# Fused attention and expert layer: the first batch's opening rearranged (64-token guess, transposes moved, one product on GpSimd)

## The chip, the cores and the metric

The kernel runs on one core of one Trainium2 chip. The metric is device time in microseconds (us), the median over several executions. The trace shown comes from one further, profiled execution on the same core.

## The reference, cut to what matters

Eight batches (B = 8) of 576 tokens go through a memory-compressed attention and then through a layer with one expert per token. All arrays are float32.

```python
a = softmax(phi, axis=memory)                  # B,H,S,M = 8,8,576,32
k_m, v_m = a^T k, a^T v                        # 32 compressed keys and values per head, head_dim 64
attn = softmax(q k_m^T / 8, axis=memory)
x = (attn v_m) laid out as tokens x 512        # 4608 x 512
expert_idx = argmax(normalised x . normalised expert_emb / tau)   # of 8 experts
out = gate * relu(x @ w1[expert]) @ w2[expert] # 512 -> 1024 -> 512
```

## The kernel before, in words

Each batch is one pass through a long pipeline, and all engines follow an order written out by hand: an instruction stands in its engine's queue where the program emits it. TensorE (PE) does transposes and products, VectorE (DVE) and ScalarE (ACT) move results out of PSUM and do the softmaxes, GpSimd (POOL) computes low-order parts and weight splits, SyncE (SP) issues loads.

**Batch 0's opening** is in `moe_linformer` (from L1059). The softmax of `phi` is transposed (`turn`), the compressed keys and values are accumulated by `slots` (L544) and scaled into `ks` by `scale` (L569). `keys` (L578) transposes the keys into `kT`, `again` (L609) copies the keys once more behind the values in `ks`, and `values` (L613) transposes what stands there into `vT`. `score` (L632) multiplies keys with queries, 32 memory slots by tokens, into PSUM tiles `ts` (the first 128 tokens) and `tr` (the rest). The second softmax is worked in blocks of 32 tokens by 32 slots, held in `x`: `fill` (L61) transposes from PSUM, `weigh` (L67) takes the maximum, subtracts and exponentiates, `divide` (L78) sums, inverts and multiplies, `turn` (L89) transposes into `aw`. All of that but the exponential is on DVE.

The expert must be known before its weights can be loaded. So the kernel guesses it in batch 0 from the first 128 tokens (`first`, blocks 0 to 3): `squares` (L637) and `products` (L672) put values times values and values times expert embeddings into `vv`; `early` (L114) gives the experts' scores of those tokens, `best` the largest, `count` (L197) the votes, and `choose` (L205) reads the winner into a register and issues the load of `w1`. Meanwhile batch 1's `phi` softmax runs, and then the remaining 448 tokens (`others`, blocks 4 to 17) go through the same second softmax. What the guess got wrong is marked by `flags` and done again by a loop at the end (`rest`, L965).

`batch(0)` (L899) then emits `keys(1)` and `values(1)`, the first half of `project` (L708: the values times `w1` give `gh`, and by subtraction its low part `gl`), the copies `part` (L690: high part `ah` by ACT, low part `al` by POOL), `attend` (L109: 40 small products on PE, then DVE reductions and the choice per token), transposes `turned` (L163) and `norm` (L172), and starts the first layer.

**The first layer** (L723) makes 16 tiles `ph`: for each, six PE matmuls over `gh·ah, gh·al, gl·ah` of two groups g, an ACT activation into `hh` and a DVE subtraction into `hl`. A `ph` tile takes one of four PSUM buffers in rotation (`mm`, L401), so PE can't begin a tile before the tile four places earlier has been read by ACT and DVE. `project` and `turned` use the same rotation. Between tiles, the lists `first[n]` and `second[n]` of `steps` (L783) say which other work is emitted: in batch 0 the second half of `project` after tile 1, `turned(3, 4)` and the count `total` after tile 2, `norm`, the loads of batch 2, and after tile 9 batch 1's `scores`, which read `kT`.

`k.warm(n)` emits n products of constants on PE whose result nobody reads.

Of the kernel before, what the change touches and what calls it, by code (L numbers as in the profile page):

```python
# [47 lines left out]
class Tokens:  # L48
# [29 lines left out]
    def divide(self, gs, ks, apart=False):  # L78
        k, nc, b = self.k, self.nc, self.b
        x = k.x[:, gs[0] : gs[-1] + 1, ks]  # L80
        n = len(gs) * (ks.stop - ks.start)
        z = k.wk.tile([P, *x.shape[1:3]], F32, tag=f"z{n}", name=f"z{b}_{gs[0]}{ks.start}")
        for i in range(len(gs)) if apart else (slice(None),):
            nc.vector.tensor_reduce(out=z[:, i], in_=x[:, i], axis=AX.X, op=ALU.add)
        nc.vector.tensor_scalar(out=z, in0=z, scalar1=1e-9, scalar2=None, op0=ALU.add)
        nc.vector.reciprocal(out=z, in_=z)
        nc.vector.tensor_tensor(out=x, in0=x, in1=z.unsqueeze(3).broadcast_to(x.shape), op=ALU.mult)

# [24 lines left out]

    def early(self, i, po):  # L114

        k, nc = self.k, self.nc
        to = slice(T0[i], T0[i] + P)
        for g in range(NG):
            nc.tensor.matmul(po[:, 144 * g : 144 * g + P + E], lhsT=k.aw[:, g, to], rhs=k.vv[:, g], start=True, stop=True)
        e = po.rearrange("p (g m) -> p g m", g=NG)[..., D : D + E]  # L120
        nc.vector.tensor_reduce(out=self.lg[:, i], in_=e.rearrange("p g e -> p e g"), axis=AX.X, op=ALU.add)
        self.best(i)

# [29 lines left out]

    def best(self, *ti):

        k, nc = self.k, self.nc
        i = slice(ti[0], ti[-1] + 1)
        nc.vector.tensor_reduce(out=self.m[:, i], in_=self.lg[:, i], axis=AX.X, op=ALU.max)
        nc.vector.tensor_tensor(
            out=self.oh[:, i], in0=self.lg[:, i], in1=self.m[:, i].unsqueeze(2).broadcast_to((P, len(ti), E)), op=ALU.is_equal  # L160
        )

# [33 lines left out]

    def count(self, key, ti):  # L197

        for i in (-1, *ti):
            self.nc.tensor.matmul(  # L200
                key, lhsT=self.k.ones, rhs=self.k.eb if i < 0 else self.oh[:, i], start=i < 0, stop=i == ti[-1]
            )
        return key

    def choose(self, ti=range(NT)):  # L205

        k, nc, b = self.k, self.nc, self.b
        if b:
            self.key = self.all = key = self.all_at_once()
        else:  # L210
            key = self.pt([P, 512], "key")
            self.spare, key = key[:, E:], key[:, :E]
            self.key = self.all = self.count(key, ti)
# [73 lines left out]
class Kernel:  # L287
# [289 lines left out]

    def keys(self, b):  # L578

        ts = [self.pt([P, NG, P], f"tk{b}_{g}") for g in range(1 if b else NG)]  # L580
        for g in range(NG):
# [30 lines left out]

    def values(self, b, gs=range(NG), copy=None):  # L613

        t = self.pt([P, NG, P], f"tv{b}_{gs[0]}")
        for g in gs:
            self.nc.tensor.transpose(t[:, g], self.ks[:, g, D:], self.ident)
        for g in gs:
            x = t[:, g].rearrange("p (k m) -> p k m", k=2)
            for i in range(2):  # L620
                r, n = slice(64 * i, 64 * i + 64), slice(32 * (i ^ g), 32 * (i ^ g) + 32)
                (copy or (self.nc.vector.tensor_copy if b > 1 or g else self.nc.scalar.copy))(self.vT[b % 2][r, g, :, n], x[r, :, n])

    def heads(self, gs=range(NG)):
# [6 lines left out]

    def score(self, b, ts, lo, hi):  # L632

        for g, j, r, c, i in self.heads():
            self.nc.tensor.matmul(ts[g][j], lhsT=self.kT[b % 2][r, g, j], rhs=self.q(b, c)[r, lo:hi], start=True, stop=True)

    def squares(self, b, ts):  # L637

        vT = self.vT[b % 2]
        self.tail = ts  # L640
        for g, j, r, c, i in self.heads():
            k = c % 2
# [140 lines left out]
    def steps(self, b, t, u):  # L783
# [7 lines left out]
        if not b:  # L791
            late = t.late()
            first[0].append(lambda: t.norm(1))
            for g in range(NG):
                first[1].append(lambda g=g: self.part(g, slice(HS, S), self.nc.scalar.copy))
            first[1] += [lambda: t.norm(2), lambda: list(self.second_part)]
            first[2] += [lambda: t.turned(3, 4), t.total]
            first[3] += [lambda: t.norm(3, 4), lambda: self.load_kv(2)]
            for f in (4, 5, 6, 7):
                first[f].append(lambda: next(late))  # L800
            first[12] += [lambda: self.keep(0), lambda: self.load_q(2)]
# [97 lines left out]
    def batch(self, b, t, u):  # L899
# [16 lines left out]
        else:  # L916
            self.keys(1)
            self.values(1, copy=self.nc.scalar.copy)
            next(project)
            self.second_part = project  # L920
            for g in range(NG):
                self.part(g, slice(P, HS), self.nc.scalar.copy)
            t.attend()
            t.turned(1, 2)
            t.norm(0)
# [133 lines left out]
def moe_linformer(ctx, tc, phiT, qT, kv, kvt, emb, tau, w1, w2, out):  # L1059
# [28 lines left out]
    for ks in ((0, 1), (4,), (2,), (3,)):  # L1088
        k.slots(0, accs, ks=ks, first=0 in ks, last=3 in ks)
        if ks[0] < 3:  # L1090
            k.warm(2 if ks[0] == 2 else 1)
    k.scale(0)
    k.load_kv(1)
    k.keys(0)
    k.again()
    first, others = slice(0, 4), slice(4, BL)
    ts = [k.mm([P, P], f"ts0_{g}", 1 + g) for g in range(NG)]
    k.score(0, ts, 0, P)
    t.fill(range(NG), first, ts)
# [12 lines left out]
    t.early(0, k.mm([P, NC * (D + E)], "po0", 2))  # L1112
    e = t.choose((0,))
    t.turned(0, pt=k.pt)
    k.largest(1, 1)
    k.softmax(1, (1,))
    k.load_q(1, (0,))
    for i in (0, 4, 8):
        k.turn(1, i, min(i + 4, 9))
        k.turns += not i  # L1120
        if not i:
# [56 lines left out]
```

## Time and profile before

| what | value |
|---|---|
| median of 3 runs | 395.6 us (394.92 to 396.23) |
| profiled execution, own time | 395.72 us |
| its span, first to last instruction | 393.9 us |
| granted TensorE clock, mean | 1.00 of full speed |
| PE busy | 384.3 us (98%) |
| DVE busy | 244.3 us (62%) |
| ACT busy | 202.7 us (51%) |
| POOL busy | 186.8 us (47%) |

Busy shares are means over the whole span; the change touches only its first tenth. The rows further down are from the trace of this execution: a time line row gives the start and the duration in us, engine, line, operation, output, input, shape and how many instructions are merged in it; in brackets stands how long the engine sat idle before it and what released it.

### The profile page before, as it was taken

To read this page: it belongs to the slowest core of one execution; us is meant where nothing else is said; L and a number is where in the kernel's file an instruction comes from. 1 tells how busy PE (TensorE), PEld (TensorE's weight loads), DVE (VectorE), ACT (ScalarE), POOL (GpSimd) and SP (SyncE) were. 2 spreads that over 40 slices of the span, in tenths; PEclk is the share of its full clock that TensorE was granted. 3 is DMA by queue.
4 is the path that set the end of the run, shared out by engine and by line. 5 is a ranking of instruction groups with operands and counts; after the bars stand their busy time and mean duration, and the time that the engine had idled before them with its cause. 6 is when DMAs were issued, how large, how long until landed. Compare 5 with 4: busy or idle time off the path is not lost. (4 is left out here: it accounts for less than half of the span.)

```text
span 393.9 us, 10292 instructions
## 1 busy us (share of the span) xinstructions
PE 384.3 (98%) x3841; PEld 310.6 (79%) x3841; DVE 244.3 (62%) x810; ACT 202.7 (51%) x625; POOL 186.8 (47%) x229
## 2 busy tenths in 40 slices
PE   7899999999999999999999999999999999999994
PEld 3458878789787987879787987879788897879882
DVE  4698894689573798348961798538951596545000
ACT  5376732166284785657656675667641751145011
POOL 1036950596153941569051961559242871529300
PEclk9999999999999999999999999999999999999999
DMA  8999956996779937995489926996369505980011
GB/s 253 344 336 381 344 152 161 322 386 262 163 216 384 406 92 181 371 376 217 88 252 353 403 79 125 350 389 248 66 162 320 203 2 106 326 317 0 30 53 43
DMA packets 68710, 91.24 MB, mean 232 GB/s; under 512 B 41160, under 2 KB 46792, under 8 KB 68528
## 3 DMA queue, kind: packets, MB, share of 16 engines
q1 hardware_dynamic: 65408, 81.35, 62.5%
q0 software_dynamic: 2688, 8.26, 5.8%
q10 hardware_dynamic: 560, 0.93, 0.9%
q8 instruction: 31, 0.51, 0.5%
q14 instruction: 23, 0.19, 0.1%
HBM read 71.19 MB, written 19.33 MB: 230 GB/s over the span
## 5 line engine op out<-in xcount | busy, mean ns | idle before, releaser
L734 PE MATMUL ph<-aT,gh 128*128 128x288 f32 x512 | 103.1, 296 | 0.0
L774 PE MATMUL py<-wh,hh 128*128 128x512 f32 x256 | 100.9, 394 | 0.0
L774 PE MATMUL py<-wl,hh 128*128 128x512 f32 x256 | 99.7, 390 | 0.0
L774 PE MATMUL py<-wh,hl 128*128 128x512 f32 x256 | 99.7, 390 | 0.0
L705 POOL TENSOR_TENSOR wl<-w2s,wh 128x512 fp32r<-128x512 f32 x64 | 83.3, 1302 | 5.1
L734 PEld LDWEIGHTS ph<-aT,gh 128*128 128x128 f32 x512 | 81.8, 188 | 1.8 <-DVE hl L741 0.8
L734 PE MATMUL ph<-aT,gl 128*128 128x288 f32 x256 | 75.4, 295 | 0.0
L738 ACT ACTIVATE hh<-ph 128x224 fp32r<-128x224 f32 (+1 forms) x128 | 48.7, 387 | 35.1 <-PE ph L734 34.6
L741 DVE SCALAR_TENSOR_TENSOR hl<-ph,hh 128x224 fp32r<-128x224 f32 (+1 forms) x128 | 51.8, 417 | 22.7 <-ACT hh L738 16.2
L779 ACT ACTIVATE ys<-py,gate 128x512 f32<-128x512 f32 (+1 forms) x40 | 25.7, 643 | 73.2 <-PE py L774 42.4
L945 POOL DMA_DIRECT2D out_dram<-ys x28 | 16.3, 582 | 92.2 <-ACT ys L779 83.5
L774 PEld LDWEIGHTS py<-wh,hh 128*128 128x128 f32 x256 | 48.1, 188 | 11.1 <-issue 1.4
L774 PEld LDWEIGHTS py<-wh,hl 128*128 128x128 f32 x256 | 48.1, 188 | 10.2
L774 PEld LDWEIGHTS py<-wl,hh 128*128 128x128 f32 x256 | 48.1, 188 | 9.4
L734 PEld LDWEIGHTS ph<-aT,gl 128*128 128x128 f32 x256 | 48.0, 188 | 0.0
L718 DVE TENSOR_TENSOR gl<-pg,gh 128x512 fp32r<-128x512 f32 x32 | 19.9, 683 | 41.1 <-ACT gh L717 41.1
L704 POOL CAST wh<-w2s 128x512 fp32r<-128x512 f32 x62 | 41.4, 668 | 0.1
L695 POOL TENSOR_TENSOR aT<-aw,aT 128x576 fp32r<-128x576 f32 (+3 forms) x20 | 23.8, 1207 | 34.0 <-DVE aT L694 27.9
L763 PE MATMUL py<-w2s,h 128*64 128x256 f32 x256 | 29.4, 382 | 0.0
L539 ACT COPY eT<-xt 32x256 f32<-32x256 f32 x64 | 25.8, 403 | 1.1
L763 PEld LDWEIGHTS py<-w2s,h 128*64 128x64 f32 x256 | 17.7, 137 | 10.4 <-DVE aw L95 1.8
L606 ACT COPY kv<-kt 32x64 f32<-32x64 f32 x80 | 19.4, 243 | 5.3 <-DVE kt L596 4.4
(168 smaller groups left out, 467.5 us busy)
## 6 DMA issues: line engine op xcount, KB each, us to landing
kx<-kv SPq DMA_DIRECT2D x32, 512.0 KB, 10.2
w2s<-w SPq DMA_DIRECT2D x28, 512.0 KB, 10.0
w1s<-w SPq DMA_DIRECT2D x28, 512.0 KB, 6.7
out_dram<-ys POOLq DMA_DIRECT2D x28, 256.0 KB, 6.3
qt<-qT SPq DMA_DIRECT2D x12, 576.0 KB, 9.5
ad<-aw SPq DMA_DIRECT2D x8, 576.0 KB, 11.4
td<-x SPq DMA_DIRECT2D x56, 72.0 KB, 2.5
ea<-td SPq DMA_DIRECT2D x7, 512.0 KB, 4.0
```

The lines of the kernel that those rows point to most:

```text
L539: nc.scalar.copy(eT[to, :8, m].rearrange("p (g k) m -> p g k m", g=NG), xt[at, :, q : BL - 2 : 4])
L606: nc.scalar.copy(y, self.kt[32 * l : 32 * l + 32, g, h + 2 * i :: 2 - 4 * i])
L695: self.nc.gpsimd.tensor_tensor(out=al, in0=a, in1=ah.bitcast(F32), op=ALU.subtract)
L704: (copy or self.nc.scalar.copy)(h, x)
L705: self.nc.gpsimd.tensor_tensor(out=l, in0=x, in1=h.bitcast(F32), op=ALU.subtract)
L718: nc.vector.tensor_tensor(out=self.gl[:, g, f], in0=ps[g], in1=self.gh[:, g, f].bitcast(F32), op=ALU.subtract)
L734: nc.tensor.matmul(p, lhsT=w[:, g, fs], rhs=x[:, g, to], start=g == 0 and k == 0, stop=g == 1 and k == 2)
L738: nc.scalar.activation(self.hh[:, f, at], q, AF.Relu)
L741: nc.vector.scalar_tensor_tensor(out=self.hl[:, f, at], in0=q, scalar=0.0, in1=self.hh[:, f, at].bitcast(F32), op0=ALU.max, op1=ALU.subtract)
L763: nc.tensor.matmul(p[64 * j : 64 * j + 64], lhsT=self.h4[:, f], rhs=self.w2s[:, f, d * j : d * j + d], start=f == 0, stop=f == 7,)
L774: nc.tensor.matmul(p, lhsT=h[:, f, to], rhs=w[:, f], start=f == 0 and k == 0, stop=f == 7 and k == 2)
L779: nc.scalar.activation(y[:, :d], p, AF.Copy, scale=gate[:, i : i + 1])
```

## The change

The first guess uses 64 tokens in place of 128, so `first` has 2 blocks and `others` 16. The keys' second copy (`again`) and the transposes of batch 0's values now stand directly behind the transposes of its keys, ahead of the scores. The router's transposes move from behind the scores to behind `slots` of the third key block, with one dummy product fewer there, and three fewer ahead of `divide`. `turned(0)` leaves the opening. `divide` of the others is emitted ahead of `again` for batch 1, and its second product (group 1) goes to GpSimd. In `batch(0)` the keys and values of batch 1 are no longer turned ahead of the first layer but after its tile 1, in one PSUM buffer of the rotation; the rest of the high and low parts (columns 64 to 288) stands ahead of `project`; `turned` and `norm` go by other token tiles and later places.

```diff
     def divide(self, gs, ks, apart=False):
...
-        nc.vector.tensor_tensor(out=x, in0=x, in1=z.unsqueeze(3).broadcast_to(x.shape), op=ALU.mult)
+        for i in parts:
+            y = x[:, i]
+            (nc.gpsimd if i == 1 else nc.vector).tensor_tensor(
+                out=y, in0=y, in1=z[:, i].unsqueeze(y.ndim - 1).broadcast_to(y.shape), op=ALU.mult
+            )
...
+    def keys_values(self, b):
+        room = self.mm([P, 2, NG, P], f"tkv{b}")
+        self.keys(b, lambda shape, name: room[:, 0])
+        self.values(b, copy=self.nc.scalar.copy, room=lambda shape, name: room[:, 1])
...
             first[0].append(lambda: t.norm(1))
             for g in range(NG):
-                first[1].append(lambda g=g: self.part(g, slice(HS, S), self.nc.scalar.copy))
-            first[1] += [lambda: t.norm(2), lambda: list(self.second_part)]
-            first[2] += [lambda: t.turned(3, 4), t.total]
-            first[3] += [lambda: t.norm(3, 4), lambda: self.load_kv(2)]
-            for f in (4, 5, 6, 7):
+                first[0].append(lambda g=g: self.part(g, slice(HS, S), self.nc.scalar.copy))
+            first[1] += [lambda: list(self.second_part), lambda: self.keys_values(1)]
+            first[3].append(lambda: self.load_kv(2))
+            first[4] += [lambda: t.turned(2, 3), lambda: t.turned(4), t.total]
+            first[5].append(lambda: t.norm(2, 3, 4))
+            for f in (5, 6, 7, 8):
                 first[f].append(lambda: next(late))
...
-            self.keys(1)
-            self.values(1, copy=self.nc.scalar.copy)
+            for g in range(NG):
+                self.part(g, slice(64, HS), self.nc.scalar.copy)
             next(project)
             self.second_part = project
-            for g in range(NG):
-                self.part(g, slice(P, HS), self.nc.scalar.copy)
             t.attend()
-            t.turned(1, 2)
+            t.turned(0, 1)
             t.norm(0)
...
         k.slots(0, accs, ks=ks, first=0 in ks, last=3 in ks)
+        if ks[0] == 2:
+            next(router, None)
         if ks[0] < 3:
-            k.warm(2 if ks[0] == 2 else 1)
+            k.warm(1)
     k.scale(0)
+    k.again()
     k.load_kv(1)
     k.keys(0)
-    k.again()
-    first, others = slice(0, 4), slice(4, BL)
-    ts = [k.mm([P, P], f"ts0_{g}", 1 + g) for g in range(NG)]
-    k.score(0, ts, 0, P)
+    k.values(0, copy=k.nc.scalar.copy)
+    first, others, few = slice(0, 2), slice(2, BL), slice(0, 64)
+    ts = [k.mm([P, 64], f"ts0_{g}", 1 + g) for g in range(NG)]
+    k.score(0, ts, 0, 64)
     t.fill(range(NG), first, ts)
-    next(router, None)
-    k.values(0, copy=k.nc.scalar.copy)
-    ts = [k.mm([P, S - P], f"tr0_{g}", g) for g in range(NG)]
-    k.score(0, ts, P, S)
-    k.squares(0, [k.pt([P, D + E], f"tl0_{g}") for g in range(NG)])
+    ts = [k.mm([P, S - 64], f"tr0_{g}", g) for g in range(NG)]
+    tl = [k.pt([P, D + E], f"tl0_{g}") for g in range(NG)]
+    for g in range(NG):
+        k.score(0, ts, 64, S, (g,))
+        k.squares(0, tl, (g,))
     list(t.weigh(range(NG), first))
     k.products(0)
-    k.warm(5, 2)
+    k.warm(2, 2)
     t.divide(range(NG), first)
     t.turn(range(NG), first)
...
-    t.early(0, k.mm([P, NC * (D + E)], "po0", 2))
-    e = t.choose((0,))
-    t.turned(0, pt=k.pt)
+    t.early(k.mm([P, NC * (D + E)], "po0", 2), few)
+    e = t.choose(few)
...
-        k.part(g, slice(0, P), k.nc.scalar.copy)
+        k.part(g, few, k.nc.scalar.copy)
...
     k.scale(1)
+    t.divide(range(NG), others, True)
     k.again(k.nc.gpsimd.tensor_copy)
-    t.divide(range(NG), others, True)
     t.turn(range(NG), others)
```

## Rows read from the trace of the kernel before

**Rows 1.** Busy time by stretch (PE, PEld, DVE, ACT, POOL, clock, DMA), first layer.

```profile
31.20:43.00 11.80, 11.80 (x135) 9.99 (x134) 9.84 (x42) 7.39 (x20) 8.70 (x12) 1.00 1.03 347
```

**Rows 2.** Page, costliest groups: one of the second layer's three products.

```profile
L774 PE MATMUL py<-wh,hh 128*128 128x512 f32 x256 | 100.9, 394 | 0.0
```

**Rows 3.** Time line, PE from batch 1's last key block to the first layer.

```profile
24.62 0.16 PEld L557 LDWEIGHTS acc0t<-kx,eT 128*32 128x32 f32 x8 [0.36 <-DMA kx<-kv]
...
26.81 0.40 PEld L582 LDWEIGHTS tk<-ident,ks 128*128 128x128 f32 x2 [0.25 <-ACT ks L574]
...
27.79 1.09 PE L715 MATMUL pg<-w1s,kv 64*32 64x512 f32 x16
...
30.07 0.73 PE L136 MATMUL po<-vv,aw 64*64 64x72 f32 x33
...
31.15 0.51 PE L734 MATMUL ph<-aT,gh 128*128 128x288 f32 x2
```

**Rows 4.** Time line, 14 to 20 us: the chain to the guess.

```profile
14.68 0.69 PE L635 MATMUL ts<-qt,kv 64*32 64x128 f32 x16
...
15.16 0.58 DVE L65 STREAM_TRANSPOSE x<-ts 128x128 f32<-128x128 f32 x2
...
15.63 0.44 PE L617 MATMUL tv<-ident,ks 128*128 128x128 f32 x2
...
16.11 0.90 ACT L622 COPY kv<-tv 64x64 f32<-64x64 f32 x4 [0.18 <-PE tv L617]
16.24 0.42 DVE L74 TENSOR_TENSOR x<-x,mx 128x256 f32<-128x256 f32 x1
...
17.03 0.42 ACT L76 ACTIVATE x<-x 128x256 f32<-128x256 f32 x1
...
19.30 0.70 PE L119 MATMUL po<-vv,aw 128*128 128x136 f32 x4 [0.50 <-DVE aw L93]
```

**Rows 5.** DVE instructions by form, to 48 us (busy us, mean ns, idle before).

```profile
L84 DVE TENSOR_REDUCE z<-x 128x14 f32<-128x448 f32 x2 | 1.1, 603 | 0.0
...
L84 DVE TENSOR_REDUCE z<-x 128x8 f32<-128x256 f32 x1 | 0.4, 421 | 0.8 <-ACT x L76 0.8
```

**Rows 6.** Time line, 25 to 31 us: the other tokens' softmax on DVE, ACT's copies.

```profile
25.42 0.17 DVE L505 RECIPROCAL rs<-rs 128x2 f32<-128x2 f32 x1 [0.38 <-POOL rs L501]
...
27.28 1.09 DVE L87 TENSOR_TENSOR x<-x,z 128x896 f32<-128x896 f32 x1
...
28.92 1.07 ACT L717 CAST gh<-pg 128x512 fp32r<-128x512 f32 x2 [0.16 <-PE pg L715]
...
29.63 0.20 DVE L95 STREAM_TRANSPOSE aw<-x 128x64 f32<-128x64 f32 x1
29.76 1.25 DVE L718 TENSOR_TENSOR gl<-pg,gh 128x512 fp32r<-128x512 f32 x2
29.88 0.56 ACT L694 CAST aT<-aw 128x160 fp32r<-128x160 f32 x2
```

**Rows 7.** Time line, 47 to 53 us: DVE and POOL with two SBUF inputs each.

```profile
47.71 0.75 DVE L74 TENSOR_TENSOR x<-x,mx 128x576 f32<-128x576 f32 x1
47.82 1.78 POOL L705 TENSOR_TENSOR wl<-w2s,wh 128x512 fp32r<-128x512 f32 x1
...
49.97 2.52 POOL L705 TENSOR_TENSOR wl<-w2s,wh 128x512 fp32r<-128x512 f32 x2
...
51.41 1.70 DVE L74 TENSOR_TENSOR x<-x,mx 128x576 f32<-128x576 f32 x1
```

**Rows 8.** Time line, the first layer's opening: DVE subtractions, moved transposes, fourth tile.

```profile
32.66 0.46 DVE L741 SCALAR_TENSOR_TENSOR hl<-ph,hh 128x288 fp32r<-128x288 f32 x1
...
34.82 0.60 PE L169 MATMUL tt<-ident,aw 128*128 128x128 f32 x4
...
35.43 0.54 PE L734 MATMUL ph<-aT,gh 128*128 128x288 f32 x2
```

**Rows 9.** Time line, PE weight loads of batch 1's scores.

```profile
41.18 0.12 PEld L635 LDWEIGHTS ts<-sT,kv 64*32 64x32 f32 x4 [0.17 <-DMA ex<-phiT]
```

More of the change, by code (lines that the diff above doesn't have):

```diff
@@ L82, in divide @@
         z = k.wk.tile([P, *x.shape[1:3]], F32, tag=f"z{n}", name=f"z{b}_{gs[0]}{ks.start}")
-        for i in range(len(gs)) if apart else (slice(None),):
+        parts = range(len(gs)) if apart else (slice(None),)
+        for i in parts:
             nc.vector.tensor_reduce(out=z[:, i], in_=x[:, i], axis=AX.X, op=ALU.add)
@@ L86, in divide @@
         nc.vector.reciprocal(out=z, in_=z)
-        nc.vector.tensor_tensor(out=x, in0=x, in1=z.unsqueeze(3).broadcast_to(x.shape), op=ALU.mult)
+        for i in parts:
+            y = x[:, i]
+            (nc.gpsimd if i == 1 else nc.vector).tensor_tensor(
+                out=y, in0=y, in1=z[:, i].unsqueeze(y.ndim - 1).broadcast_to(y.shape), op=ALU.mult
+            )
     def turn(self, gs, ks):
@@ L112, in attend, with early @@
         self.pairs()
-    def early(self, i, po):
+    def early(self, po, to):
         k, nc = self.k, self.nc
-        to = slice(T0[i], T0[i] + P)
         for g in range(NG):
[L119 to L122, printed above, removed]
+            nc.tensor.matmul(po[to, 144 * g : 144 * g + P + E], lhsT=k.aw[:, g, to], rhs=k.vv[:, g], start=True, stop=True)
+        e = po[to].rearrange("p (g m) -> p g m", g=NG)[..., D : D + E]
+        nc.vector.tensor_reduce(out=self.lg[to, 0], in_=e.rearrange("p g e -> p e g"), axis=AX.X, op=ALU.add)
+        self.best(0, to=to)
     def open(self):
@@ L152, in pairs, with best @@
         self.best(*range(NT))
-    def best(self, *ti):
+    def best(self, *ti, to=slice(P)):
         k, nc = self.k, self.nc
         i = slice(ti[0], ti[-1] + 1)
[L158 to L161, printed above, removed]
+        lg, m = self.lg[to, i], self.m[to, i]
+        nc.vector.tensor_reduce(out=m, in_=lg, axis=AX.X, op=ALU.max)
+        nc.vector.tensor_tensor(out=self.oh[to, i], in0=lg, in1=m.unsqueeze(2).broadcast_to(lg.shape), op=ALU.is_equal)
     def turned(self, *ti, pt=None):
@@ L195, in all_at_once, with count, choose @@
         return key
[L197 to L202, printed above, removed]
+    def count(self, key, to):
+        self.nc.tensor.matmul(key, lhsT=self.k.ones, rhs=self.k.eb, start=True, stop=False)
+        self.nc.tensor.matmul(key, lhsT=self.k.ones[to], rhs=self.oh[to, 0], start=False, stop=True)
         return key
-    def choose(self, ti=range(NT)):
+    def choose(self, to=None):
         k, nc, b = self.k, self.nc, self.b
@@ L212, in choose @@
             self.spare, key = key[:, E:], key[:, :E]
-            self.key = self.all = self.count(key, ti)
+            self.key = self.all = self.count(key, to)
         ki = k.wk.tile([1, 1], I32, tag="ki", name=f"ki{b}")
@@ L576, in scale, with keys @@
                 self.nc.vector.tensor_scalar(out=to, in0=self.accs[g], scalar1=r, scalar2=None, op0=ALU.mult)
-    def keys(self, b):
-        ts = [self.pt([P, NG, P], f"tk{b}_{g}") for g in range(1 if b else NG)]
+    def keys(self, b, room=None):
+        ts = [(room or self.pt)([P, NG, P], f"tk{b}_{g}") for g in range(1 if b else NG)]
         for g in range(NG):
@@ L611, in again, with values @@
         (copy or self.nc.vector.tensor_copy)(self.ks[:, :, 2 * D :], self.ks[:, :, :D])
-    def values(self, b, gs=range(NG), copy=None):
-        t = self.pt([P, NG, P], f"tv{b}_{gs[0]}")
+    def values(self, b, gs=range(NG), copy=None, room=None):
+        t = (room or self.pt)([P, NG, P], f"tv{b}_{gs[0]}")
         for g in gs:
@@ L630, in heads, with score, squares @@
                 yield g, slice(l, l + 32), slice(64 * i, 64 * i + 64), c, slice(n, n + 32)
-    def score(self, b, ts, lo, hi):
-        for g, j, r, c, i in self.heads():
+    def score(self, b, ts, lo, hi, gs=range(NG)):
+        for g, j, r, c, i in self.heads(gs):
             self.nc.tensor.matmul(ts[g][j], lhsT=self.kT[b % 2][r, g, j], rhs=self.q(b, c)[r, lo:hi], start=True, stop=True)
-    def squares(self, b, ts):
+    def squares(self, b, ts, gs=range(NG)):
         vT = self.vT[b % 2]
         self.tail = ts
-        for g, j, r, c, i in self.heads():
+        for g, j, r, c, i in self.heads(gs):
             k = c % 2
@@ L1119, in moe_linformer @@
         k.turn(1, i, min(i + 4, 9))
-        k.turns += not i
+        k.turns += i == 4
         if not i:
```

## The prediction

> **What bounds the kernel now.** I first read the busy time by stretch. From the first layer on, PE has no free time: 11.80 us busy in the 11.80 us from 31.20 on, at the full granted clock (1.00, the 2.4 GHz level) [rows 1], and the second layer's products have no idle time ahead of them [rows 2]. So the change can gain only by starting the first layer earlier, and each PE instruction that it carries past that start costs its own time.
>
> The second view is the time line of PE ahead of that start [rows 3]. At 24.62 PE waits for batch 1's last key block. After its products and ACT's scaling come the transposes of keys and values (26.81 to 27.79), the first half of `project` (27.79), the products of `attend`, and tile 0 at 31.15. PE has one wait worth naming here: the products of group 1 go on at 30.07, and what they need is DVE's last transpose, ended at 29.63 + 0.20 = 29.83 [rows 3, 6]. Two chains thus end together: PE's from the key block, and DVE's through the other tokens' softmax. Moving batch 1's transposes shortens the first by 27.79 - 26.81 = 0.98 us, so PE alone allows tile 0 at 30.17. The second must be shortened as well, and that I work out next. From DVE's end to tile 0 it is 31.15 - 29.83 = 1.32 us, the same work before and after (four transposes of tokens, the rest of `attend`).
>
> **The guess chain, from 14.7 us.** The reader is to see in [rows 4] that the scores start at 14.68, the fills at 15.16, and that the exponential starts at 17.03 although the subtraction ended at 16.24 + 0.42 = 16.66: ACT was copying values until 16.11 + 0.90 = 17.01. After the change the value transposes (0.44) stand ahead of the scores, partly in PE's wait for the copied keys; I take 0.25 of delay (ends 0 and 0.44). Scores of half the width give back some 0.08, the two fills of 64 columns 0.09 each (0.58 for two of 128 against 0.20 for one of 64 [rows 4, 6]), so the maximum starts when it did. The price per element is (603 - 421) / 192 = 0.95 ns [rows 5]; maximum, subtraction, sum, product and exponential each lose 128 elements, 0.12 us, 0.6 together. The wait behind the value copies (0.37) goes, because those copies now lie ahead of the fills. The transposes into `aw` give 0.09. Sum: 1.05 us earlier (ends 0.8 and 1.1); PE's `early` products go from 19.30 to 18.25. The dropped dummy products stood in PE's waits; the router's transposes take the place of one of them while PE waits for a key block, so both are costed at nothing (cover gone: some 0.4 us for the four).
>
> **The other tokens' chain.** Everything DVE does next is queued behind it and moves up by 1.05. But 64 more elements per group pass through two fills, maxima, subtractions and sums: 8 x 0.06 = 0.5 us. Of DVE's wait of 0.38 for POOL's part of the row sums [rows 6] I take 0.15 as gone (ends 0 and 0.38), since DVE arrives later relative to POOL. The product then starts at 27.28 - 1.05 + 0.5 - 0.15 = 26.6.
>
> What is a product on POOL worth? [rows 7] show the two engines shutting each other out when both have two SBUF inputs: POOL's split needs 2.52 / 2 = 1.26 but 1.78 when DVE's subtraction is running, and went on for 1.14 after that ended (48.46 to 49.60); DVE's subtraction needs 0.75 but 1.70 when it meets POOL's. The change's two products are of just that kind and become ready at the same reciprocal. DVE has no semaphore to wait for and should be first: 0.42 + 256 x 0.95 ns = 0.66, to 27.25. POOL's follows, to 28.4. DVE meanwhile turns group 0 (one turn is (29.83 - 28.37) / 2 = 0.73, plus 0.06 for the added columns, 0.79, to 28.05), waits 0.35 for POOL, and turns group 1 until 29.2. With both products on DVE it would be 26.6 + 1.21 + 2 x 0.79 = 29.4. So the move to POOL is worth 0.2 us, and if the engines did not exclude each other POOL would be done at 27.9 and DVE at 28.85.
>
> The Trainium skill ("GPSIMD Engine Reference", sections 1, Specifications, and 4.1, Engine selection) names contention with VectorE instructions of two SBUF inputs and advises VectorE for elementwise two-input work, GpSimd being about twice as slow. By that advice the sum would stand at 29.4 in place of 29.2; the trace agrees on the contention (1.70 against 0.75 us) and here the advice is worth less than nothing only because DVE has transposes to do meanwhile.
>
> DVE's end thus moves from 29.83 to 29.2, tile 0 from 31.15 to **30.55, 0.6 us earlier** (ends 0.98, PE's own limit above, and a delay of 0.3, the POOL rival below).
>
> **What is carried past the start.** Six transposes now lie in the PE-bound part: two each of keys and values, and the two of the token tile that the opening used to turn. Four cost 0.60 busy [rows 8], 0.15 each at the most; since runs overlap I take 0.11 each: **+0.65** (ends 0.4, if some fall into waits, and 0.9). ACT's copies, the norms and POOL's splits move too; their engines have idle time per tile, and where that fails is a rival below.
>
> **New waits.** ACT now has the two `part` copies (0.28 each for 160 columns) queued ahead of the `gh` copies (0.54 each) [rows 6], and the second of them waits for DVE's last large transpose, at about 29.0. So `gh` of group 0 is ready at 29.9 and DVE, which went straight from its transposes to `gl` at 29.76, sits idle for 0.7. `gl` ends at 31.15 against 29.76 + 1.25 = 31.01; behind it are queued the reductions of `attend`, `norm(0)` and `hl` of tile 0, which goes from 32.66 to 32.8. Tile 0 itself is 0.6 earlier, so PE meets buffers that DVE hasn't released: I take **+0.2** of waiting for tile 2's buffer (ends 0 and 0.8). On the other side the scores of batch 1 wait 0.17 for a load [rows 9]; they now come later and the load is issued earlier: **-0.17** (ends 0 and -0.17).
>
> **Sum.** -0.6 + 0.65 + 0.2 - 0.17 = +0.1 us against the profiled execution's 395.72 (span 393.9 and 1.8 around it, 0.1 above the median of 395.6): **395.8 us**, no change. About 0.3%, 1.2 us, is what a measurement of this kernel can tell from none.
>
> **Rivals.**
> - *Faster.* The opening gains all that PE allows (-0.98), because my DVE prices are too high or the engines share better than in [rows 7], and the six transposes and the buffer waits cover each other (0): -0.98 - 0.17 = -1.15, 394.5 us. For it: DVE at 28.85 without exclusion would make PE's limit the later one. Against it: PE showed no waits in the first layer that transposes could fill [rows 1].
> - *Slower: ACT becomes the bound of tiles 2 to 5.* The copies of batch 1's keys and values move into the layer behind two wide `part` copies and two `gh` copies. They are four value copies of 0.90 together [rows 4] and one key copy of about 0.37 (0.28 for 160 columns, 96 more at the price of 0.95 ns [rows 5, 6]). If ACT has no idle time there, `hh` of tile 2 is late by all of it, 1.27 us, and PE stands still at the tile four places on: 395.8 + 1.27 = 397.1. It decides if `hh` of tile 2 ends later than PE reaches tile 6. Against it: the rotation leaves four tiles of slack.
> - *POOL first.* If POOL's product gets the shared input ahead of DVE's, DVE's starts 1.26 later: DVE's end is 26.6 + 1.26 + 0.66 + 1.58 = 30.1, 0.9 later than forecast, and the time 396.7. For it: the release is the same instant. Against it: in [rows 7] the engine already running kept it, and DVE is in sequence.
> - *The guess fails.* If 64 tokens named another expert than 128, batch 0 would be done again by the closing loop, about (393.9 - 31.15) / 8 = 45 us. The second layer's 256 products are 8 batches by 4 full tiles by 8 slices [rows 2], so no batch was repeated and all tokens of a batch go to one expert; 64 tokens give the same one.
>
> **How the numbers follow.** The forecast has 0.46 (its own range 395.1 to 396.6), the faster rival 0.2, ACT 0.21, POOL first 0.12, the failed guess 0.01. The faster rival is centred on the bound of 0.3%, so I count 0.16 as faster; of ACT's case all but 0.02 is beyond it on the other side, and POOL first adds 0.02 with the higher price of the transposes: slower 0.22, same 0.62. The range that leaves out two in ten reaches from 394.4 into the faster case to 397.3 with ACT's.
>
> **What would show it.** Right: `early` on PE near 18.25; POOL's product starting when DVE's ends and lasting to about 28.4; DVE's last `aw` transpose ending near 29.2; tile 0 near 30.55 with the clock still at 1.00; tile 5 at about the time it had before. Wrong: tile 0 earlier than 30.2 or later than 31.2; a PE wait over 0.5 us between tiles 2 and 6; any second-layer product beyond 256.

## The result and the profile after

The change made the kernel slower: a median of 398.3 us (396.82 to 398.51, 6 runs) against 395.68 us (394.92 to 396.51, 6 runs), a ratio of 1.0057 with a 95% interval of 1.0037 to 1.0077. A second series, e7 below, gave 397.89 us (12 runs) against 396.33 us, 1.0046 (1.0026 to 1.0066). The forecast was 395.8 us with a range to 397.3; the result lies above it.

The profiled execution took 397.67 us, its span is 395.9 us. I start where the forecast started, with the first layer's stretch by busy time (columns: PE, PEld, DVE, ACT, POOL, granted clock, DMA share, GB/s), here of the changed kernel:

```profile
31.20:43.00 11.80, 10.70 (x117) 8.93 (x123) 7.42 (x33) 7.82 (x23) 8.56 (x11) 1.00 1.04 357
```

PE, busy all of this stretch before [rows 1], now has 1.1 us without work, at the same clock. The list of PE's waits from the end of the opening to the second layer (in total, times, longest, us) says where:

```profile
PE tkv L618 <- ACT kv L588: 1.1, 1, 1.1
PE pg L722 <- DMA w1s<-w: 0.3, 1, 0.3
PE po L140 <- issue: 0.2, 1, 0.2
PE py L770 <- DVE hl L748: 0.2, 1, 0.2
```

The largest stands inside the new function. The time line of the changed kernel around it:

```profile
32.97 0.44 PE L583 MATMUL tkv<-ident,ks 128*128 128x128 f32 x2
33.10 1.07 ACT L724 CAST gh<-pg 128x512 fp32r<-128x512 f32 x2 [0.46 <-PE pg L722]
...
34.06 0.39 ACT L588 COPY kv<-tkv 128x256 f32<-128x256 f32 x1
...
34.51 0.20 PEld L618 LDWEIGHTS tkv<-ident,ks 128*128 128x128 f32 x2 [1.34 <-ACT kv L588]
34.51 0.44 PE L618 MATMUL tkv<-ident,ks 128*128 128x128 f32 x2 [1.10 <-ACT kv L588]
...
34.70 0.51 PE L741 MATMUL ph<-aT,gh 128*128 128x288 f32 x2
```

Keys are transposed at 32.97. The values' transposes go into the same PSUM buffer, and the program has ACT's copy of the keys (L588) between the two; so they wait for that copy, and in ACT's queue it stands behind both `gh` copies. Tile 2 follows at 34.70, 4.51 us after tile 0; before it was 2.77 us (31.15 to 33.92), without that wait:

```profile
33.92 0.53 PE L734 MATMUL ph<-aT,gh 128*128 128x288 f32 x2
```

The opening, in the same time line:

```profile
12.73 0.35 DVE L577 TENSOR_SCALAR ks<-acc0t,rs 128x128 f32<-128x128 f32 x1 [1.31 <-PE acc0t L558]
...
17.31 0.65 PE L123 MATMUL po<-vv,aw 128*64 128x136 f32 x4
...
25.45 0.69 DVE L90 TENSOR_TENSOR x<-x,z 128x512 f32<-128x512 f32 x1
25.50 1.55 POOL L90 TENSOR_TENSOR x<-x,z 128x512 f32<-128x512 f32 x1 [0.60 <-DVE z L87]
...
26.82 1.09 PE L722 MATMUL pg<-w1s,kv 64*32 64x512 f32 x16 [0.35 <-DMA w1s<-w]
...
27.72 0.20 DVE L100 STREAM_TRANSPOSE aw<-x 128x64 f32<-128x64 f32 x1
...
29.25 0.60 PE L140 MATMUL po<-vv,aw 64*64 64x72 f32 x22 [0.19 <-issue]
...
30.19 0.51 PE L741 MATMUL ph<-aT,gh 128*128 128x288 f32 x2
```

These times can't be set against those of before as they stand. The scaling of batch 0's keys, the first of these rows, starts anywhere from 12.73 to 14.98 us in the 13 profiles of this document, and the rest of the opening moves with it; in the kernel before it starts at

```profile
13.59 0.35 DVE L576 TENSOR_SCALAR ks<-acc0t,rs 128x128 f32<-128x128 f32 x1 [1.35 <-PE acc0t L557]
```

I therefore count the opening from that instruction. `early` then comes 5.71 us after it before (19.30 - 13.59) and 4.58 after: 1.13 earlier. DVE's last transpose ends 16.24 after it before and 15.19 after (27.92 - 12.73): 1.05 earlier. But tile 0 comes 17.56 after it before and 17.46 after: 0.1 earlier. The gain that DVE made stopped ahead of PE.

The one other place that differs is far behind, in batch 1's second layer of the changed kernel:

```profile
106.52 1.72 PE L558 MATMUL acc<-kx,eT 128*32 128x128 f32 x51
108.77 0.64 PE L558 MATMUL acc<-kx,eT 128*32 128x128 f32 x13 [0.53 <-issue]
```

From the half tile ahead of this to the next batch's first projection the changed kernel took 24.76 us (101.51 to 126.27), the kernel before 23.86 (100.42 to 124.28): 0.9 us in a wait that the profile ascribes to nothing. The half tile that ends the first layer starts, first in the changed kernel, then in the kernel before, at

```profile
48.53 3.67 PE L770 MATMUL py<-w2s,h 128*64 128x256 f32 x32 [0.16 <-DVE hl L748]
```

```profile
47.43 3.67 PE L763 MATMUL py<-w2s,h 128*64 128x256 f32 x32
```

The balance of the two spans: tile 0 at 30.19 against 31.15 (-0.96, of which 0.86 is the early arrival), tile 0 to the half tile 18.34 us against 16.28 (+2.06), this wait (+0.9): +2.0, the difference of 395.9 and 393.9.

### The profile page after: what moved, and what is told of

The parts are those of the page before. It is cut to its first block, busy times and chain, and to the rows that moved or that the text cites. A ratio compares the mean times of both kernels' runs of the same rounds, so it can differ in the third digit from the quotient of the medians.

```text
span 395.9 us, 10286 instructions
## 1 busy us (share of the span) xinstructions
PE 384.5 (97%) x3837; PEld 310.4 (78%) x3837; DVE 243.1 (61%) x810; ACT 202.8 (51%) x625; POOL 188.2 (48%) x230
```

## The experiments

The table holds, for each kernel's profile, the start of batch 0's scaling, of the first half of `project`, of tile 0 and of the half tile that ends the first layer; "opening" is from scaling to tile 0, "layer" from tile 0 to the half tile. The last column is the ratio to the kernel before, timed with it on the same chip. Each row is one profiled execution. Two pairs have the same order in the opening, the changed kernel and e7, e6 and e9: their openings differ by 0.59 and 0.30 us, and the time from scaling to `project` by 0.67 and 0.69. A smaller difference between two openings is thus no finding. The layer repeats far better: 18.34, 18.35 and 18.35 in the changed kernel, e7 and e4.

| kernel | scaling | project | tile 0 | half tile | opening | layer | ratio (95%) |
|---|---|---|---|---|---|---|---|
| before | 13.59 | 27.79 | 31.15 | 47.43 | 17.56 | 16.28 | 1 |
| changed | 12.73 | 26.82 | 30.19 | 48.53 | 17.46 | 18.34 | 1.0057 (1.0037 to 1.0077) |
| changed, again (e7) | 14.00 | 27.42 | 30.87 | 49.22 | 16.87 | 18.35 | 1.0046 (1.0026 to 1.0066) |
| e1 transposes first | 13.59 | 27.47 | 31.60 | 48.94 | 18.01 | 17.34 | 1.001 (0.9995 to 1.0024) |
| e2 old place | 13.31 | 28.28 | 31.13 | 47.92 | 17.82 | 16.79 | 1.0017 (1.0003 to 1.0031) |
| e3 move alone | 14.98 | 28.97 | 32.54 | 50.38 | 17.56 | 17.84 | 1.0035 (1.001 to 1.0061) |
| e4 product on DVE | 13.09 | 26.88 | 30.32 | 48.67 | 17.23 | 18.35 | 1.0048 (1.0026 to 1.0069) |
| e5 PE stream shifted | 13.62 | 27.18 | 32.93 | 50.26 | 19.31 | 17.33 | 1.0051 (1.0029 to 1.0072) |
| e6 old place, again first | 13.19 | 27.39 | 30.78 | 47.42 | 17.59 | 16.64 | 1.0001 (0.9983 to 1.002) |
| e8 guess alone | 13.96 | 28.48 | 31.35 | 48.12 | 17.39 | 16.77 | 1.001 (0.9993 to 1.0026) |
| e9 e6, old tiles | 13.37 | 28.26 | 31.26 | 47.96 | 17.89 | 16.70 | 1.0001 (0.9988 to 1.0015) |
| e10 before, less load | 12.79 | 26.70 | 31.14 | 47.41 | 18.35 | 16.27 | 0.9989 (0.9974 to 1.0004) |
| e11 e6, less load | 13.47 | 26.59 | 29.98 | 47.10 | 16.51 | 17.12 | 0.9983 (0.9969 to 0.9997) |

**e1: the four transposes ahead of their copies.** Same buffer, same instructions, another order on PE.

```diff
     def keys_values(self, b):
-        room = self.mm([P, 2, NG, P], f"tkv{b}")
-        self.keys(b, lambda shape, name: room[:, 0])
-        self.values(b, copy=self.nc.scalar.copy, room=lambda shape, name: room[:, 1])
+        nc, room = self.nc, self.mm([P, 2, NG, P], f"tkv{b}")
+        for n, c in enumerate((slice(0, 2 * D), slice(D, 3 * D))):
+            for g in range(NG):
+                nc.tensor.transpose(room[:, n, g], self.ks[:, g, c], self.ident)
+        nc.scalar.copy(self.kT[b % 2], room[:, 0])
...
```

> The changed kernel, but batch 1's four transposes of keys and values are issued before any copy out of their shared PSUM buffer. Theory A (the values' transposes stand behind ACT's copy of the keys, which stands behind the two gh copies): PE's wait of 1.10 us ahead of them goes, tile 2 starts some 3.4 us after tile 0 instead of 4.5, and the time falls by about 1.1 us to 397.2. Rival B (ACT is the bound of these tiles, the wait only moves to the next buffer): less than 0.3 us is won, PE waits for hh or hl at tiles 2 to 6 instead. The wait of 0.5 to 0.9 us in batch 1's second layer (behind the 51st of 64 key products, near 108 us) is untouched by either.

The layer went from 18.34 to 17.34 us, by 1.00, and the time to 1.001 of before, from 1.0046 and 1.0057. In the time line the four transposes run without a break, and the next tile follows while ACT is still busy with `gh`:

```profile
34.38 0.66 PE L630 MATMUL tkv<-ident,ks 128*128 128x128 f32 x4
34.52 1.08 ACT L731 CAST gh<-pg 128x512 fp32r<-128x512 f32 x2 [0.47 <-PE pg L729]
34.79 0.51 PE L748 MATMUL ph<-aT,gh 128*128 128x288 f32 x2
...
35.47 0.39 ACT L631 COPY kv<-tkv 128x256 f32<-128x256 f32 x1
```

This is theory A. ACT copies the keys as late as before, 3.87 us after tile 0 in both kernels, and PE doesn't wait for it; so rival B, ACT as the bound, falls. The time, 396.76 us, is 0.4 below what theory A gave. Separate buffers for keys and values, with the order left as it was, would test the same from the other side; that was not run. The profile holds a wait that is not in theory A, and it hides part of the gain in this one execution:

```profile
30.66 0.60 PE L140 MATMUL po<-vv,aw 64*64 64x72 f32 x22 [0.96 <-issue]
```

Within `attend` (40 products, which leave 80 rows in the trace) PE stops behind the 58th row, where the changed kernel stops for 0.19 us; see e5.

**e2: batch 1's keys and values in their old place.**

```diff
-            first[1] += [lambda: list(self.second_part), lambda: self.keys_values(1)]
+            first[1] += [lambda: list(self.second_part)]
...
+            self.keys(1)
+            self.values(1, copy=self.nc.scalar.copy)
             for g in range(NG):
                 self.part(g, slice(64, HS), self.nc.scalar.copy)
             next(project)
```

> The changed kernel with batch 1's keys and values turned ahead of the first half of project again, as before; all else as changed. Theory A: the 1.10 us wait and 0.4 us of transposes leave the first layer, while tile 0 starts up to 1.0 us later; net 0.5 to 1.2 us faster than the changed kernel, 397.1 to 397.8. Rival C (the opening is bound by DVE or by the w1 load, not by PE): tile 0 starts no more than 0.4 us later, and the time is 396.7 or less. Rival B: no change, 398.3.

396.49 us, below what theory A gave and in the range of rival C: the layer is 1.55 us shorter than the changed kernel's, while the opening is 0.4 to 0.95 us longer (17.82 against 17.46 and 16.87). So the move buys the opening less than it costs the layer. The opening also has a wait of its own making:

```profile
26.08 1.55 POOL L90 TENSOR_TENSOR x<-x,z 128x512 f32<-128x512 f32 x1 [0.60 <-DVE z L87]
27.58 0.28 POOL L612 COPY ks<-ks 128x128 f32<-128x128 f32 x1
27.91 0.44 PE L618 MATMUL tv<-ident,ks 128*128 128x128 f32 x2 [0.83 <-POOL ks L612]
```

The keys' second copy (L612) stands behind POOL's product in POOL's queue, and PE's value transposes wait for it. In the changed kernel the same copy is late too, but nothing needs it before the first layer.

**e3: the move alone, in the kernel before.**

```diff
...
-            self.keys(1)
-            self.values(1, copy=self.nc.scalar.copy)
             next(project)
...
-            first[1] += [lambda: t.norm(2), lambda: list(self.second_part)]
+            first[1] += [lambda: t.norm(2), lambda: list(self.second_part), lambda: self.keys_values(1)]
```

> The kernel before, with nothing but batch 1's keys and values moved behind tile 1 in one buffer, as in the change. Theory A: DVE's chain still sets tile 0 (31.15), the first layer gains 0.4 us of transposes and a wait of about 1 us: 397.1, 1.4 us slower than before. Rival C: tile 0 moves up by what PE is relieved of (0.98) and the time stays within 0.5 us of before. Rival B: as A, but with waits for hh spread over tiles 2 to 6.

397.74 us against 396.22: 1.5 us slower, as theory A had it. The layer grew by 1.56 us and the opening is the same 17.56. Two waits stand in its trace:

```profile
28.97 1.09 PE L721 MATMUL pg<-w1s,kv 64*32 64x512 f32 x16 [0.81 <-DMA w1s<-w]
...
36.85 0.44 PE L617 MATMUL tkv<-ident,ks 128*128 128x128 f32 x2 [1.10 <-ACT kv L587]
```

The second is that of the changed kernel. The first shows where the 0.98 us went by which the move relieves PE ahead of `project`: PE waits 0.81 of it for `w1`. The move alone costs 1.0035, its interval reaching to 1.0061, the whole change 1.0046 and 1.0057: about as much, so the rest of the change comes to little.

**e4: both products on DVE.**

```diff
-            (nc.gpsimd if i == 1 else nc.vector).tensor_tensor(
+            nc.vector.tensor_tensor(
```

> The changed kernel with both second products of divide on DVE. Theory: in the changed kernel tile 0 waits for the load of w1 and the products behind it, not for DVE's last transposes, so 0.2 to 0.5 us more on DVE is hidden: 398.3, no change. Rival D (POOL's product buys what it looks like, because DVE's opening sets tile 0 and its hl): 0.3 to 0.8 us slower, 398.6 to 399.1. The wait near 108 us tells, by being there or not, whether it is a matter of this one profile.

1.0048 against 1.0046 and 1.0057: no difference. The products and the last transpose on DVE are here

```profile
25.97 1.29 DVE L90 TENSOR_TENSOR x<-x,z 128x512 f32<-128x512 f32 x2
...
28.53 0.20 DVE L100 STREAM_TRANSPOSE aw<-x 128x64 f32<-128x64 f32 x1
```

From the first product's start to DVE's end it is 2.76 us (25.97 to 28.73) against 2.47 with POOL's product (25.45 to 27.92), so the product on POOL frees 0.29 us on DVE, and tile 0 doesn't come later for lack of it: the opening, 17.23 us, lies between the two of the changed kernel. Rival D falls. With the same order on PE, batch 1's second layer has no wait near 108 us here.

**e5: 24 tiny products ahead of `early`.** Added to e1, where PE is idle.

```diff
+    tiny = k.mm([P, 4], "tiny", 2)
+    for _ in range(24):
+        k.nc.tensor.matmul(tiny, lhsT=k.ones, rhs=k.ones[:, :4], start=True, stop=True)
     t.early(k.mm([P, NC * (D + E)], "po0", 2), few)
```

> The kernel of the reordered transposes (batch 1's four transposes ahead of their copies) with 24 tiny products of constants added on PE ahead of early, where PE is idle. Theory P (the wait behind the 58th of the 80 rows of attend, 0.96 us there and released by nothing the profile shows, hangs on the place in PE's instruction stream): with 48 instructions more ahead of it the wait leaves attend and falls on the last key products of batch 1, where PE waits for w1 anyway; tile 0 starts 0.2 to 1.0 us earlier relative to the first products' arrival, time 396.0 to 396.7. Rival Q (it is a hidden dependency of those products): the wait stays behind the 58th row and the time is the same, 396.8, or later by the 24 products' 0.6 us.

```profile
28.21 0.87 PE L140 MATMUL po<-vv,aw 64*64 64x72 f32 x34
31.61 0.97 PE L140 MATMUL po<-vv,aw 64*64 64x72 f32 x46 [2.53 <-issue]
```

The wait moved from behind the 58th to behind the 34th row, by exactly the 24 products. So it hangs on the place in PE's stream, as theory P says, and not on those products' data, as rival Q says; but theory P's gain did not come, since the wait stayed inside `attend` (I had counted two places per added product) and grew to 2.53 us. The time rose from 1.001 to 1.0051 of before. The 2.53 us are of an execution of 399.56 us, 1.6 above the median of this kernel; how long the others stop is not known.

**e6: as e2, with the copy ahead of POOL's product.**

```diff
+    k.again(k.nc.gpsimd.tensor_copy)
     t.divide(range(NG), others, True)
-    k.again(k.nc.gpsimd.tensor_copy)
```

> The changed kernel with batch 1's keys and values turned in their old place, and the copy of the keys (again) ahead of POOL's product, as before the change. Theory: in the run with the old place alone PE's value transposes waited 0.8 us for that copy, which stood behind POOL's 1.55 us product; this wait goes, the first half of project starts 0.8 us earlier, tile 0 0.3 to 0.5 us earlier, time about 396.1, level with before. Rival: POOL's product now starts later and DVE's last transposes with it, so tile 0 does not move: 396.5.

The 0.83 us wait is gone, `project` starts 14.20 us after the scaling against 14.97 in e2, and the time is level with before (1.0001). `project` starts as long after the scaling as in the kernel before (27.79 - 13.59 = 14.20; in e9, the same opening once more, 14.89): the opening has gained nothing. POOL's product now starts when DVE's has ended, and takes 1.05 us:

```profile
26.93 1.05 POOL L90 TENSOR_TENSOR x<-x,z 128x512 f32<-128x512 f32 x1
...
28.41 1.10 PE L140 MATMUL po<-vv,aw 64*64 64x72 f32 x54
29.72 0.71 PE L140 MATMUL po<-vv,aw 64*64 64x72 f32 x26 [0.21 <-issue]
```

PE stops within `attend` here too, behind the 54th row: four rows earlier than in the changed kernel, and the four transposes of keys and values now stand ahead of `attend`. That is a second sign for theory P.

**e7: the changed kernel again.** No edit.

> The changed kernel once more, on the chip of the other runs. If the 0.9 us between the third batch's start and its predecessor (behind the 51st key product, near 108 us) belongs to the kernel, it is there again; if it is chance of one execution, batch 1's second layer takes 45.2 us from half tile to half tile as in every other profile. The 1.10 us wait for the key copy must be there in either case. Time 397.5 to 398.3.

```profile
35.19 0.44 PE L618 MATMUL tkv<-ident,ks 128*128 128x128 f32 x2 [1.10 <-ACT kv L588]
```

The wait for the key copy is there, 1.10 us again, and the layer takes 18.35 us. The wait near 108 us is not: from half tile to the next projection it is 23.90 us (102.19 to 126.09). So 0.9 us of the first profile's span is chance of one execution. It is not of the changed kernel alone: e8 stops behind the same 51st row, and takes 24.40 us there (101.10 to 125.50). The time, 397.89, lies in the expected band. Tile 0 comes 16.87 us after the scaling, 0.59 earlier than in the first profile, and as much earlier `w1` has landed: its load takes

```profile
w1s<-w SPq DMA_DIRECT2D x2, 1024.0 KB, 5.9
```

against 6.5 there.

**e8: the guess alone.** e2 with e4's edit.

> Of the change only the 64-token guess, the values behind the keys and the later token transposes: keys and values of batch 1 in their old place, both products on DVE. Theory: PE's chain from batch 1's keys sets tile 0 as in the kernel before, so a guess 1.2 us earlier buys 0 to 0.4 us, and two more token transposes and later norms in the first layer cost 0.3 to 0.5: level with before, 396.2 to 396.5. Rival (the early guess is worth its 1.2 us): 395.2 or less.

396.82 us against 396.33, a ratio whose interval takes in 1; the time is 0.3 above the expected band. The opening is 17.39 us, 0.17 less than before and so within what one profile can tell, the layer 16.77, 0.49 more. The rival, that the guess is worth its 1.2 us, falls.

**e9: e6 with the layer's side work in about its old tiles.**

```diff
-                first[0].append(lambda g=g: self.part(g, slice(HS, S), self.nc.scalar.copy))
-            first[1] += [lambda: list(self.second_part)]
-            first[3].append(lambda: self.load_kv(2))
-            first[4] += [lambda: t.turned(2, 3), lambda: t.turned(4), t.total]
-            first[5].append(lambda: t.norm(2, 3, 4))
-            for f in (5, 6, 7, 8):
+                first[1].append(lambda g=g: self.part(g, slice(HS, S), self.nc.scalar.copy))
+            first[1] += [lambda: list(self.second_part)]
+            first[2].append(lambda: t.turned(2, 3))
+            first[3] += [lambda: t.turned(4), t.total, lambda: t.norm(2, 3), lambda: self.load_kv(2)]
+            first[4].append(lambda: t.norm(4))
+            for f in (4, 5, 6, 7):
```

> The kernel with the 64-token guess, POOL's product and batch 1's keys and values in their old place and again ahead of the product; in addition the first layer's side work goes back to about its old tiles (part after tile 1, turned after tiles 2 and 3, norm after 3 and 4, late from 4). Theory: of the 0.4 us by which its first layer was longer than before, the two more token transposes (0.2) stay and the late gate work (0.2) goes: 396.0. Rival: nothing changes, 396.2.

395.87 against 395.74, 1.0001; the layer is 16.70 us, not 16.4. The rival has the sum right: nothing is won. The parts did change. Behind batch 1's scores the layer is back at 5.25 us (42.71 to 47.96, from the `squares` behind the scores to the half tile), as before (42.17 to 47.43), against 5.57 in e6 (41.85 to 47.42), and PE no longer waits for the last `hl`. Ahead of the scores it takes 0.38 more than e6 (31.26 to 42.71, 11.45, against 30.78 to 41.85, 11.07).

**e10 and e11: half a load less.** Batch 1's key and value rows 256 to 511 are not loaded; batch 0's stay in their place, so batch 1's output is computed from a mixture. e10 is the kernel before, e11 is e6.

```diff
-            for k in range(4):
+            for k in range(2 if b == 1 else 4):
                 self.nc.sync.dma_start(self.kx[k], self.kv[b, :, k])
```

> The kernel before without half of batch 1's load of keys and values: token blocks 2 and 3 of 4 keep batch 0's rows, so the output of batch 1 is another. 1 MB less stands ahead of w1 in the load stream. Theory L (the opening is set by loads: batch 1's last key block, then w1 behind it): the last key product no longer waits, the first half of project starts up to 1.5 us earlier, until PE's own order or the guess (w1 asked for at 22.2) sets it; tile 0 0.3 to 1.0 us earlier relative to the start of batch 0's scaling. Rival M (DVE sets it): tile 0 stays 17.56 us behind that scaling.

> The same omission (token blocks 2 and 3 of batch 1 keep batch 0's rows) in the kernel with the early guess and again ahead of the product. Theory L: with the loads out of the way the guess's 1.2 us now counts, since w1 is asked for at 20.8 and lands in about 5.3 us: tile 0 0.7 to 1.3 us earlier than in the kernel before with the same omission, and 1 us or more earlier than without it. Rival M: the gap between the two kernels stays what it is with all loads, 0 to 0.2 us.

```profile
30.06 0.73 PE L136 MATMUL po<-vv,aw 64*64 64x72 f32 x33 [0.91 <-issue]
```

This row is of e10. `project` starts 13.91 us after the scaling in e10 and 13.12 in e11, against 14.20 in the kernel before, 14.20 in e6 and 14.89 in e9, which have all loads. So the kernel with the early guess starts `project` 1.1 to 1.8 us sooner with half a load gone, more than the scatter of two profiles, and the load does stand in its way. The 0.3 by which e10 is sooner than the kernel before, and the 0.8 between e10 and e11, are not clear of that scatter. Tile 0 is 1.84 us earlier in e11 than in e10, of which 0.91 is the wait above, which e11 hasn't got; 0.93 remain, within what theory L gave, from one profile of each. e10's own tile 0 is no earlier than before, 17.44 without that wait, so there L's lower figure was missed: PE's and DVE's chains lie close behind the load. And of e11's 0.93 the layer takes back 0.85 (17.12 against 16.27): 0.36 is what e6's layer has too, and the rest is PE waiting for `gl` in the first two tiles, which take 2.25 us (29.98 to 32.23) against 1.76 in e6 (30.78 to 32.54). The times, 395.4 and 394.97, don't separate.

## Why the prediction was wrong

**The guess chain: right.** Forecast 1.05 us earlier, measured 1.13 from the scaling to `early`, in both profiles of the changed kernel. The exponential's wait behind the value copies went.

**The other tokens' chain and POOL's product: right in kind, too small.** DVE's end was forecast 0.6 us earlier and came 1.05 earlier. The two products did exclude each other all but fully, DVE first: of POOL's 1.55 us from 25.50 on, 0.91 come after DVE's product ended at 26.14, where POOL's alone takes 1.05 (e6); DVE's took 0.69, and 0.65 each with both on DVE (e4). The forecast had 1.14 there, from [rows 7]. Its worth on DVE is 0.29 us, not 0.2 (e4), and none of it reaches the time. The Trainium skill ("GPSIMD Engine Reference", 4.1, Engine selection) advises VectorE for an elementwise product; e4 does that, and it cost nothing.

**Tile 0 0.6 us earlier: wrong in its mechanism.** It came 0.1 earlier in one profile and 0.69 in the other (e7); that the second is near 0.6 is luck. The step that failed is "from DVE's end to tile 0 it is 1.32 us, the same work before and after". It became 2.27 us (27.92 to 30.19) and 1.68 in e7 (29.19 to 30.87), because DVE no longer ended last. From then on tile 0 hangs on `w1`, for which `project` waits 0.35 us at 26.82 and 0.31 in e7, and on PE's way from there. The prediction has no term for this load. `w1` is asked for at 22.23 before and at 20.16 after, counted from the scaling 1.21 us earlier (8.64 and 7.43), but the load takes as much longer. The issues in the time line and in the list of DMA issues (issue to landing, median us), first of before, then of the changed kernel:

```profile
22.23 1.40 SPq L460 DMA_DIRECT2D w1s<-w  x2
w1s<-w SPq DMA_DIRECT2D x2, 1024.0 KB, 5.3
```

```profile
20.16 1.40 SPq L461 DMA_DIRECT2D w1s<-w  x2
w1s<-w SPq DMA_DIRECT2D x2, 1024.0 KB, 6.5
```

Its first half lands 13.94 us after the scaling before (22.23 + 5.3 - 13.59) and 13.93 after; in e7, with 5.9, it is 13.33. From `project` to tile 0 it then takes 3.37 us (26.82 to 30.19), and took 3.36 before. That is not all work. Where nothing stops PE within `attend`, as in e2, it is 2.85 (28.28 to 31.13):

```profile
29.30 1.48 PE L140 MATMUL po<-vv,aw 64*64 64x72 f32 x80
```

So 0.5 us of the way are stops. Before, the longer one is that at 30.07, which the prediction put down to DVE's last transpose; PE went on 0.24 us after its end, where in e3 it goes on 0.06 after the transpose that it waits for (30.45 to 30.51), so DVE need not account for all of it. In the changed kernel DVE had been done for 0.9 us when PE stopped behind the 58th row; see the last section.

Before, the load stream had a gap ahead of `w1` (last two columns, DMA share and GB/s, of the kernel before):

```profile
22.00:23.00 1.00, 1.00 (x7) 0.43 (x5) 1.00 (x3) 1.00 (x3) 0.13 (x1) 1.00 0.62 238
23.00:24.00 1.00, 1.00 (x18) 0.77 (x21) 1.00 (x3) 0.67 (x2) 0.76 (x4) 1.00 0.48 113
```

and in the changed kernel it doesn't:

```profile
22.00:23.00 1.00, 0.59 (x24) 0.25 (x12) 1.00 (x3) 0.51 (x3) 0.94 (x2) 1.00 0.97 354
23.00:24.00 1.00, 0.20 (x8) 0.00 (x0) 0.89 (x3) 1.00 (x3) 0.44 (x1) 1.00 1.05 399
```

The gap was closed; asked for earlier, `w1` now moves in a stream that is full, and in the first of the two profiles it lands no earlier. With batch 1's keys in their old place `project` stands behind that batch's last key block, which PE awaits for 0.88 us in e6 and which comes 11.03 us after the scaling there (13.19 to 24.22) as before (13.59 to 24.62 in [rows 3]).

**What is carried past the start: right.** Forecast 0.65 for six transposes. The four of keys and values lengthen e1's layer by 0.55 over e2's; with 0.2 for the two of tokens (below) it is 0.75.

**New waits, +0.2: the step that failed and decided the time.** I looked for waits at the buffers that `hl` frees and at the tile four places on, and put ACT's added copies into a rival of that kind. The wait that came stands inside the moved step: its own second half waits for the copy of its first half, 1.10 us, at the place in ACT's queue behind two `gh` copies of 1.07 together. It is in every kernel that moves the step as written (the changed kernel twice, e3, e4) and goes, with 1.00 us of layer, when the transposes are issued first (e1). The ACT rival's price (1.27) and sign were near the result, its mechanism was another: e1 leaves ACT's work as it is. That the price came near is luck.

**The scores' load wait, -0.17: not there.** The 0.17 us ahead of the scores are 0.16 now, and the profile no longer names a load; it wasn't the load.

```profile
41.99 0.12 PEld L642 LDWEIGHTS ts<-sT,kv 64*32 64x32 f32 x4 [0.16 <-issue]
```

**The sum.** Opening -0.1 to -0.7, layer +2.06: 1.4 to 2.0 us, where the two series measured 2.6 and 1.6. Of the layer's 2.06 the key copy is 1.0, the moved transposes of keys and values 0.55, and 0.5 stays when both are undone (e2). About 0.2 of that lies ahead of the scores (31.13 to 42.34 in e2, 11.21, against 31.15 to 42.17, 11.02), where the two more token transposes stand. The other 0.3 lies between the `squares` behind the scores and the half tile (42.34 to 47.92, 5.58, against 5.26), where PE waits for the last `hl`; the changed kernel has the same (42.98 to 48.53, 5.55). In e9, with the side work in about its old places, this 0.3 is gone, but as much is lost ahead of the scores. What stays open is the time that the profiles don't hold: the changed kernel's medians, 398.3 and 397.89, lie 0.6 and 0.4 above its profiled executions. Stops like the 0.9 us near 108 us, which 2 of the 13 profiles show, may be part of it; that was not measured.

No version with all its loads was faster than the kernel before. The best of the parts, e6 and e9, are level with it.

## What to carry to other kernels

When a step is moved into a busy stretch, read it as its own little chain: if its second half must wait for another engine's copy of its first half, it takes that engine's queue with it, and issuing all of its PE work ahead of the copies may be worth more than the move. A chain that ends in a load's request pays, when shortened, only as far as the load stream has room; look for the gap in the stream's GB/s and count no more than that. Where two chains end together, add up each from its last common event to the end, since the time from one chain's end to the goal holds only as long as that chain is the later one.

## What was not expected

PE's waits "issue" in `attend` follow the place in PE's instruction stream. They stand behind row 47 in the order of the kernel before (e10, 0.91 us), behind row 58 in that of the changed kernel (0.19, e1 0.96), behind row 54 with keys and values back in their place (e6, 0.21) and behind row 34 with 24 products added (e5, 2.53). The change issues ten rows fewer ahead of `attend` (four dummy products, two token transposes, four of keys and values), which is about the step from 47 to 58. In [rows 3] the wait at 30.07, which the profile puts down to DVE, is behind the same 47th row.

In e1's window around the wait, 27 to 31 us, the DMA view shows a packet of the kind "instruction" in queue 8, among a stream that has no free time:

```profile
q1 hardware_dynamic: 527, 1.44, 100.8%
q8 instruction: 1, 0.02, 1.5%
```

The traces hold each packet's own start and length. Every one of the 13 has one such packet of 16 KB between 26 and 31 us, and wherever PE stops in `attend` with nothing named, it goes on 1.3 to 1.5 us after that packet has ended; so it does near 108 us:

| kernel | packet ends | PE goes on | behind row |
|---|---|---|---|
| before | 28.75 | 30.07 | 47 |
| changed | 27.90 | 29.25 | 58 |
| e1 | 29.26 | 30.66 | 58 |
| e5 | 30.08 | 31.61 | 34 |
| e6 | 28.39 | 29.72 | 54 |
| e10 | 28.53 | 30.06 | 47 |
| changed, batch 1 | 107.47 | 108.77 | 51 |
| e8, batch 1 | 106.60 | 107.99 | 51 |

Where PE runs past the place without such a wait (e2, e8 and e11 in `attend`), the packet had ended at least 1.4 us earlier. So the stop looks like PE waiting for its next instructions, fetched through the same busy engines. The times fit that closely, but no run moved the packet alone, and what it carries isn't in the trace; it is argued, not shown. What is shown is that a change of a few products ahead of `attend` moves the stop along PE's stream, and that between 0.2 and 2.5 us were lost there in one execution or another.
